# Q/K/V projections per quarter of the heads, and a prologue that runs under attention, in a fused attention and token-MLP kernel

## The chip, the cores and the metric

The kernel runs on one core of one Trainium2 chip. The metric is the device time of one execution in microseconds (us). All runs compared here are marked fast in the record, and each lists one core.

## The reference, cut to what matters

```python
xn = layernorm(x)                                    # x: [1, 2048, 512], bf16
# A: attention with 32 heads of width 16
q, k, v = split(xn @ wqkv)                           # wqkv: [512, 3*512]
o = softmax(q @ k.T * 16**-0.5) @ v                  # per head, 2048 x 2048 scores
a = o @ wo
# B: token MLP, along the 2048 tokens, with width F = 1376
h = layernorm(xn)
u = gelu(h.T @ w1 + b1)                              # tanh form
b = (u @ w2 + b2).T
out = x + a + b
```

The scores have 32 * 2048 * 2048 = 134 million elements, and each needs an exponential. That is the work which cannot be made smaller here.

## The kernel before

All engines get their instruction streams from one scheduling loop in Python. Scores are computed transposed (keys on partitions). One *period* of the loop is one key tile of 128 keys for 4 heads and 512 queries: four score matmuls that use 32 rows of TensorE each, two exponentials of 128x1024 on ScalarE, and four PV matmuls for the period two before. Sixteen periods make a *block* (4 heads, 512 queries), and there are 32 blocks. Scores go to three PSUM slots of two banks each, bank 6 takes PV, and bank 7 (`EX_BANK`) takes every other matmul: projections, MLP and output projection. Such extra work is queued, and each period takes up to `EXTRA_BUDGET` matmuls from the queue; a task that asks for more at once, as a Q projection with its 4, is taken whole when the period has taken nothing else yet.

```python
EXTRA_BUDGET = 3.0
...
for s_ in range(NT + 4):                 # prologue, 16 tiles of 128 tokens
    if s_ < NT:
        ln_stats(s_, 0)
        ...
    t = s_ - 1
    if 0 <= t < NT:
        ln_norm(t, 0); transpose_pe(t, t % 2)
    t = s_ - 2
    if 0 <= t < NT:
        transpose_copy(t, t % 2, "act")
        v_pe(t, 2 + (t % 2))             # V of all 32 heads
        if t % 4 == 3:
            kt_pe(0, t // 4, ...)        # K of head-quarter 0
    ...                                  # evacuations of stage s_ - 3
qt_block(0, EX_BANK, evac_eng="act")
...
def task_qt(b):                          # Q of one block: a burst of four matmuls
    yield 4.0                            # weights padded with zeros per head parity
    qt_block(b, EX_BANK)
...
while True:                              # one period
    score_group(period)                  # 4 matmuls into slots n % 3
    exp_pair(2 * period); exp_pair(2 * period + 1)
    pv_group(...)                        # of period - LAG
    ...                                  # extra work: at most EXTRA_BUDGET matmuls
```

After the last block, its head group is copied from PSUM, its denominators are broadcast and inverted in four pieces, and each piece is multiplied, projected, added and stored before the next is inverted.

The softmax here doesn't subtract the row's maximum and nothing guards it: scores larger than these inputs give would overflow.

Of the kernel before, what the change touches and what calls it, by code (L numbers as in the profile page):

```python
# [13 lines left out]
D = 512  # L14
# [18 lines left out]
EXTRA_BUDGET = 3.0  # L33
# [23 lines left out]
class Sched:  # L57
# [11 lines left out]
    def add(self, eng, fn, reads=(), writes=(), name="", dma=False, extra_deps=(), out_dma=False):  # L69
# [4 lines left out]
        for k in reads:  # L74
            w = self.last_writer.get(k)
            if w is not None:
                deps.add(w)
        for k in writes:
            w = self.last_writer.get(k)
            if w is not None:  # L80
                deps.add(w)
            for r in self.readers.get(k, ()):
                deps.add(r)
# [97 lines left out]
def bass_parallel_sum__softmax_full_mha__mixer_token_mlp__prompt_kernel(  # L181
# [18 lines left out]
    with ExitStack() as es:  # L200
# [18 lines left out]
        wq_pad = sb("wq_pad", [128, NCT, NG, 128], BF16)  # L219
# [54 lines left out]
        v17_main = V17[:, 0:NKT * H * 17].rearrange("p (n c) -> p n c", c=17)  # L274
        sc.add("dve", lambda e: e.memset(v17_main[:, :, 16:17], 1.0), writes=[("Vone",)])
        sc.add("dve", lambda e: e.memset(V17[:, NKT * H * 17:], 0.0), writes=[("Vpad",)])

        xsplits = [(0, 1), (1, 2), (2, 4), (4, 8), (8, 12), (12, 16)]
        for (a, b_) in xsplits:
            dma("sp", x_sb[:, a:b_, :],  # L280
                x2[128 * a:128 * b_, :].rearrange("(t p) d -> p t d", p=128),
                reads=[], writes=[("x", t) for t in range(a, b_)], name="ld_x")
            if a == 0:
                dma("sp", wqkv_sb[:], A_wqkv.rearrange("(ct p) n -> p ct n", p=128),
                    reads=[], writes=[("wqkv",)], name="ld_wqkv")
# [8 lines left out]

        def pool_wqpad_piece(i):
            if i < NCT:
                sc.add("pool", lambda e: e.memset(wq_pad[:, i, :, :], 0.0), writes=[("wq_pad_ct", i)])
            else:
                j = i - NCT
                e_, ct = divmod(j, NCT)  # L300
                src = wqkv_sb[:, ct, 0:D].rearrange("p (T r e d) -> p T r e d", T=4, r=4, e=2)[:, :, :, e_, :]
                dst = wq_pad[:, ct, :, :].rearrange("p (T e) (r f d) -> p T e r f d", e=2, r=4, f=2)[:, :, e_, :, e_, :]
                sc.add("pool", lambda e, dst=dst, src=src: e.tensor_copy(dst, src),
                       reads=[("wqkv",), ("wq_pad_ct", ct)], writes=[("wq_pad_ct", ct)] +
                       ([("wq_pad", g) for g in range(NG)] if j == 2 * NCT - 1 else []), name="wqpad")
# [58 lines left out]
        def kt_evac(T, c, bk, evac_eng):  # L364
            evac(evac_eng, KT[:, T, 512 * c:512 * (c + 1)], bank(bk), reads=[("bank", bk)], writes=[("KT", T, c)])

        def kt_pe(T, c, bk):
            for ct in range(NCT):
                sc.add("pe", lambda e, ct=ct: e.matmul(  # L369
                    bank(bk), lhsT=wqkv_sb[:, ct, D + 128 * T: D + 128 * T + 128],  # L370
                    rhs=xnT[:, ct, 512 * c:512 * (c + 1)], start=(ct == 0), stop=(ct == NCT - 1)),
                    reads=[("wqkv",)] + [("xnT", t) for t in range(4 * c, 4 * c + 4)], writes=[("bank", bk)])
# [6 lines left out]
        def qt_block(b, bk, evac_eng="dve"):  # L379
            qb, G = divmod(b, NG)  # L380
            slot = b % NQS
            for ct in range(NCT):
                sc.add("pe", lambda e, ct=ct: e.matmul(  # L383
                    bank(bk), lhsT=wq_pad[:, ct, G, :], rhs=xnT[:, ct, 512 * qb:512 * (qb + 1)],
                    start=(ct == 0), stop=(ct == NCT - 1)),
                    reads=[("wq_pad", G)] + [("xnT", t) for t in range(4 * qb, 4 * qb + 4)], writes=[("bank", bk)])
            evac(evac_eng, QT[:, slot, :], bank(bk), reads=[("bank", bk)], writes=[("QT", slot)])

        def v_tile(t, bk, evac_eng="dve"):
            v_pe(t, bk)  # L390
            v_evac(t, bk, evac_eng)

        def v_evac(t, bk, evac_eng):
            dst = V17[:, t * H * 17:(t + 1) * H * 17].rearrange("p (h c) -> p h c", c=17)[:, :, 0:16]
            src = bank(bk).rearrange("p (h d) -> p h d", d=16)
            evac(evac_eng, dst, src, reads=[("bank", bk)], writes=[("V", t)])

        def v_pe(t, bk):
            for ct in range(NCT):
                sc.add("pe", lambda e, ct=ct: e.matmul(  # L400
                    bank(bk), lhsT=xnT[:, ct, 128 * t:128 * (t + 1)], rhs=wqkv_sb[:, ct, 2 * D:3 * D],
                    start=(ct == 0), stop=(ct == NCT - 1)),
                    reads=[("wqkv",), ("xnT", t)], writes=[("bank", bk)])

        pool_piece = 0
        for s_ in range(NT + 4):
            if s_ < NT:
                ln_stats(s_, 0)
                if pool_piece < 3 * NCT:
                    pool_wqpad_piece(pool_piece)  # L410
                    pool_piece += 1
            t = s_ - 1
            if 0 <= t < NT:
                ln_norm(t, 0)
                transpose_pe(t, t % 2)
            t = s_ - 2
            if 0 <= t < NT:
                transpose_copy(t, t % 2, "act")
                v_pe(t, 2 + (t % 2))
                if t % 4 == 3:  # L420
                    kt_pe(0, t // 4, 4 + ((t // 4) % 2))
            t = s_ - 3
            if 0 <= t < NT:
                v_evac(t, 2 + (t % 2), "dve" if t % 2 == 1 else "act")
                if t % 4 == 3:
                    kt_evac(0, t // 4, 4 + ((t // 4) % 2), "act")
        while pool_piece < 3 * NCT:
            pool_wqpad_piece(pool_piece)
            pool_piece += 1
        qt_block(0, EX_BANK, evac_eng="act")  # L430
        late_consts()

        def task_ln2():
            for t in range(NT):
                yield 0.0
                ln_tile(t, 1)

        def task_qt(b):
            yield 4.0
            qt_block(b, EX_BANK)  # L440

        def task_kt(T):
            for c in range(4):
                yield 4.0
                kt_chunk(T, c, EX_BANK)
# [61 lines left out]
        def task_outproj(qb, sti):  # L507
# [3 lines left out]
            ng = NG - 1 if lastqb else NG  # L511
            for G in range(ng):
                yield 1.0
                sc.add("pe", lambda e, G=G: e.matmul(  # L514
# [17 lines left out]
        def final_tile(qb, sti):  # L532
            st = 4 * qb + sti
            par = qb % 2
            G = NG - 1
            bk = sti
            sc.add("pe", lambda e: e.matmul(
                bank(bk), lhsT=oT[:, par, G, 128 * sti:128 * (sti + 1)], rhs=wo_pad[:, G, :],
                start=True, stop=True),
                reads=[("oTc", par, G, sti), ("wo_pad", G)], writes=[("bank", bk)])  # L540
            final_store(st, bk)
            yield 0.0
# [6 lines left out]
        def task_epilogue_rest(b):  # L549
            qb, G = divmod(b, NG)  # L550
            eb = b % 2
            last = (b == NBLK - 1)
# [3 lines left out]
            for c in range(4):  # L556
# [4 lines left out]
                if last:  # L561
                    sc.add("dve", lambda e, cs=cs: e.tensor_tensor(oT[:, qb % 2, G, cs], OT32[:, eb, cs],
                                                                   denb[:, eb, cs], ALU.mult),
                           reads=[("OT32", eb), ("denb", eb, c)], writes=[("oTc", qb % 2, G, c)])
                    for _ in final_tile(qb, c):
                        pass
            if not last:
                yield 0.0
                sc.add("pool", lambda e: e.tensor_tensor(oT[:, qb % 2, G, :], OT32[:, eb, :], denb[:, eb, :], ALU.mult),  # L569
                       reads=[("OT32", eb)] + [("denb", eb, c) for c in range(4)],  # L570
                       writes=[("oTc", qb % 2, G, c) for c in range(4)])
# [9 lines left out]
        def score_group(g):  # L581
            b, kt, qb, G, T, e_ = blk_of(g)
            slot_q = b % NQS
            for r in range(4):
                n = 2 * g + r // 2
                s_ = n % 3
# [5 lines left out]
                    reads=[("KT", T, kt // 4), ("QT", slot_q)], writes=[("bank", bk)], name="sc")  # L592

        def exp_pair(n):
            s_ = n % 3
# [4 lines left out]
        def pv_group(g):  # L600
            b, kt, qb, G, T, e_ = blk_of(g)
            for r in range(4):
# [8 lines left out]
                    reads=[("V", kt), ("pT", buf), ("Vone",)] + ([("V", kt + 1)] if kt + 1 < NKT else [("Vpad",)]),  # L611
# [4 lines left out]

        sched_list = []
        for b in range(1, NBLK):
            sched_list.append((P(b - 1, 1), 0, "qt", b))
        for T in range(1, 4):  # L620
            sched_list.append((P(2 * T - 2, 2), 1, "kt", T))
        for ft in range(NFT):
            sched_list.append((P(1, 4) + 6 * ft, 2, "ut", ft))
        for st in range(NT):
            sched_list.append((P(1, 4) + 6 * NFT + 7 * st, 3, "yt", st))
        for qb in range(NQB):
            for sti in range(4):
                if qb < NQB - 1:
                    sched_list.append((P(8 * (qb + 1), 8) + 4 * sti, 4, "op", (qb, sti)))
                else:  # L630
                    sched_list.append((P(NBLK - 1, 8) + 2 * sti, 4, "op", (qb, sti)))
        sched_list.sort(key=lambda z: (z[0], z[1]))

        def start_task(kind, arg):
            if kind == "qt":
                return task_qt(arg)
            if kind == "kt":
                return task_kt(arg)
            if kind == "ut":
# [18 lines left out]
        free_tasks = [Task("ln2", None, task_ln2())]  # L658
# [5 lines left out]
        while True:  # L664
            if period == P(0, 8):
# [123 lines left out]
```

## Time and profile before

| what | before | where it is read |
|---|---|---|
| median time | 1042.1 us (4 runs), 1041.07 (13 runs) | timing runs |
| span of the profiled run | 1040.3 us | page |
| ScalarE busy | 967.0 us (93%) | page, part 1 |
| start of the first exponential | 44.43 us | ScalarE's timeline |
| ScalarE idle ahead of exponentials | 32.0 us | groups |
| end of the last exponential to the end | 15.1 us | ScalarE's timeline |

Lines of the page of the kernel before: busy time by engine, the clock row (the span in 40 slices, tenths of full clock), the chain of waits by engine and by line, and the group of the exponentials (busy us, mean ns of one | idle us ahead of them, and what ended it).

```profile
PE 893.7 (86%) x4833; PEld 211.2 (20%) x4896; DVE 294.9 (28%) x476; ACT 967.0 (93%) x1065; POOL 75.7 (7%) x116
PEclk9966888887899999965557755555555955555558
ACT 78%; PE 14%; DVE 4%; issue 1%; POOL 1%; DMA 1%; ACTq 0%; SPq 0%
L597 ACT ACTIVATE pT<-ps 128x1024 bf16<-128x1024 f32 x1024 | 946.4, 1255 | 32.0 <-PE ps L588 32.0
```

ScalarE is the limit (busy 967.0 of 1040.3 us). So the time is a sum along ScalarE: the start of the first exponential, the exponentials, the gaps between them, and what follows the last one. The mean of 1255 ns is the length of one record; records overlap, and back to back one starts every 0.92 us (32 take 29.44 us in the timeline below).

ScalarE's timeline of the kernel before shows the sum's terms (start us, duration us, group of adjacent instructions, and in brackets the idle time ahead and who ended it).

```profile
44.43 9.38 ACT L597 ACTIVATE pT<-ps 128x1024 bf16<-128x1024 f32 x10 [0.48 <-PE ps L588]
...
293.41 159.60 ACT L597 ACTIVATE pT<-ps 128x1024 bf16<-128x1024 f32 x174 [0.44 <-PE ps L588]
453.87 29.44 ACT L597 ACTIVATE pT<-ps 128x1024 bf16<-128x1024 f32 x32 [0.85 <-PE ps L588]
484.16 29.44 ACT L597 ACTIVATE pT<-ps 128x1024 bf16<-128x1024 f32 x32 [0.85 <-PE ps L588]
...
1014.09 11.11 ACT L597 ACTIVATE pT<-ps 128x1024 bf16<-128x1024 f32 x12 [0.55 <-PE ps L588]
```

From about 450 us on there is a gap of 0.85 us behind 16 of the 18 Q bursts, one burst per block of 32 exponentials, while in the 159.60 us before that there is none. The table of windows of the kernel before (window, its length; busy us and count of PE, PEld, DVE, ACT, POOL; then PEclk, DMA share, GB/s):

```profile
300.00:350.00 50.00, 46.28 (x293) 13.12 (x299) 17.74 (x28) 50.00 (x56) 2.54 (x2) 1.00 0.19 44
600.00:650.00 50.00, 45.12 (x216) 8.67 (x218) 10.83 (x16) 48.28 (x53) 2.53 (x2) 0.50 0.00 1
```

With MLP matmuls among the scores (300 to 350 us) the granted clock is 1.00, without them (600 to 650 us) 0.50. TensorE's timeline of the kernel before, around 451 us, shows what the Q burst does on the slow clock (0.50 from 450.8 to 453.3 us):

```profile
450.85 0.61 PE L607 MATMUL ps<-pT,V 128*32 128x512 bf16 x4
451.80 1.49 PE L383 MATMUL ps<-xnT,wq_pad 128*128 128x512 bf16 x3 [0.33 <-issue]
453.22 1.03 PE L588 MATMUL ps<-QT,KT 32*128 32x512 bf16 x6
```

L383 is the Q burst (one of its four records is missing). It stands between the PV matmuls and the next scores (L588), which start at 453.22; the next exponential could only start at 453.87, after its gap.

### The profile page before, as it was taken

To read this page: it belongs to the slowest core of one execution; us is meant where nothing else is said; L and a number is where in the kernel's file an instruction comes from. 1 tells how busy PE (TensorE), PEld (TensorE's weight loads), DVE (VectorE), ACT (ScalarE), POOL (GpSimd) and SP (SyncE) were. 2 spreads that over 40 slices of the span, in tenths; PEclk is the share of its full clock that TensorE was granted. 3 is DMA by queue.
4 is the path that set the end of the run, shared out by engine and by line. 5 is a ranking of instruction groups with operands and counts; after the bars stand their busy time and mean duration, and the time that the engine had idled before them with its cause. 6 is when DMAs were issued, how large, how long until landed. Compare 5 with 4: busy or idle time off the path is not lost.

```text
span 1040.3 us, 11570 instructions
## 1 busy us (share of the span) xinstructions
PE 893.7 (86%) x4833; PEld 211.2 (20%) x4896; DVE 294.9 (28%) x476; ACT 967.0 (93%) x1065; POOL 75.7 (7%) x116
## 2 busy tenths in 40 slices
PE   5777887888889999889988899888898899898895
PEld 2311221222222222211112211111111211111111
DVE  6654433343332223322201222221022222102214
ACT  3698999999999999999999999999999999999994
POOL 5431000000000000000000000000000000000000
PEclk9966888887899999965557755555555955555558
DMA  5020201011012111100000000000000000000000
GB/s 141 19 44 21 48 21 41 21 22 35 1 29 51 37 29 42 28 0 1 1 1 11 11 1 1 1 1 1 1 0 6 16 1 1 1 1 1 1 1 20
DMA packets 54372, 18.31 MB, mean 18 GB/s; under 512 B 49200, under 2 KB 53808, under 8 KB 54320
## 3 DMA queue, kind: packets, MB, share of 16 engines
q1 hardware_dynamic: 54320, 17.58, 7.1%
q8 instruction: 38, 0.62, 0.2%
q14 instruction: 14, 0.11, 0.0%
HBM read 15.47 MB, written 2.10 MB: 17 GB/s over the span
## 4 chain that ended last, share of the span: by engine, by line
ACT 78%; PE 14%; DVE 4%; issue 1%; POOL 1%; DMA 1%; ACTq 0%; SPq 0%
ACT pT L597 77%; PE ps L588 4%; PE ps L383 3%; PE ps L607 2%; PE ps L468 1%; DVE stats L323 1%; PE ps L400 1%; DVE big L338 1%; POOL mv L329 1%; PE ps L514 1%; DMA x_sb<-in_A_x_dram 1%; ACT ga_sb L483 1%; PE ps L369 1%; DVE mv L325 0%; PE ps L348 0%
## 5 line engine op out<-in xcount | busy, mean ns | idle before, releaser
L597 ACT ACTIVATE pT<-ps 128x1024 bf16<-128x1024 f32 x1024 | 946.4, 1255 | 32.0 <-PE ps L588 32.0
L588 PE MATMUL ps<-QT,KT 32*128 32x512 bf16 x2048 | 482.7, 511 | 99.7 <-ACT pT L597 65.4
L607 PE MATMUL ps<-pT,V 128*32 128x512 bf16 x2048 | 262.1, 514 | 2.2 <-DVE OT L546 1.9
L588 PEld LDWEIGHTS ps<-QT,KT 32*128 32x128 bf16 x2048 | 94.0, 96 | 510.7 <-ACT pT L597 461.4
L546 DVE COPY OT<-ps 128x512 f32<-128x512 f32 x32 | 22.1, 691 | 436.4 <-PE ps L607 436.3
L559 DVE RECIPROCAL denb<-denb 128x128 f32<-128x128 f32 x128 | 110.3, 915 | 0.9
L569 POOL TENSOR_TENSOR oT<-OT,denb 128x512 bf16<-128x512 f32 x31 | 39.3, 1267 | 880.9 <-DVE denb L559 880.9
L607 PEld LDWEIGHTS ps<-pT,V 128*32 128x32 bf16 x2048 | 53.0, 99 | 169.6 <-issue 166.4
L468 PE MATMUL ps<-big,w1blk 128*128 128x512 bf16 (+1 forms) x165 | 54.2, 434 | 2.5 <-issue 1.8
L383 PE MATMUL ps<-xnT,wq_pad 128*128 128x512 bf16 x101 | 43.2, 558 | 7.8 <-issue 7.8
L495 PE MATMUL ps<-gT,w2blk 128*128 128x512 bf16 (+1 forms) x165 | 47.1, 386 | 2.3 <-issue 1.9
L514 PE MATMUL ps<-wo_pad,oT 128*128 128x512 bf16 x115 | 36.0, 415 | 2.0 <-issue 1.8
L377 DVE CAST QT<-ps 128x512 bf16<-128x512 f32 x31 | 21.4, 691 | 35.9 <-PE ps L383 35.9
L500 DVE SCALAR_TENSOR_TENSOR big<-ps,x_sb 128x512 f32<-128x512 f32 x16 | 11.0, 690 | 66.9 <-PE ps L495 66.9
L473 DVE TENSOR_SCALAR u_sb<-ps,b1col 128x512 f32<-128x512 f32 (+1 forms) x11 | 8.2, 750 | 73.3 <-PE ps L468 73.3
L527 DVE TENSOR_TENSOR osb<-ps,big 128x512 bf16<-128x512 f32 x16 | 11.1, 691 | 57.7 <-PE ps L514 55.1
L376 ACT ACTIVATE xnT<-ps 128x512 bf16<-128x512 bf16 x16 | 9.5, 594 | 16.7 <-PE ps L348 16.7
L554 DVE STREAM_SHUFFLE denb<-OT 128x512 f32<-128x512 f32 x32 | 23.1, 721 | 0.0
L348 PE MATMUL ps<-ident,big 128*128 128x128 bf16 x64 | 7.4, 249 | 15.3 <-DVE big L338 15.2
L369 PE MATMUL ps<-xnT,wqkv_sb 128*128 128x512 bf16 x61 | 17.1, 397 | 3.9 <-DVE KT L377 3.2
L468 PEld LDWEIGHTS ps<-big,w1blk 128*128 128x128 bf16 (+1 forms) x176 | 14.0, 105 | 28.6 <-issue 20.5
L400 PE MATMUL ps<-wqkv_sb,xnT 128*128 128x512 bf16 x62 | 19.6, 450 | 0.1
(44 smaller groups left out, 205.1 us busy)
## 6 DMA issues: line engine op xcount, KB each, us to landing
w1blk<-in_B_w_dram SPq DMA_DIRECT2D x10, 512.0 KB, 4.1
w2blk<-in_B_w_dram SPq DMA_DIRECT2D x16, 320.0 KB, 3.3
out_dram<-osb SPq DMA_DIRECT2D x16, 128.0 KB, 1.7
wqkv_sb<-in_A_wqkv_dram SPq DMA_DIRECT2D x1, 1536.0 KB, 6.8
x_sb<-in_A_x_dram SPq DMA_DIRECT2D x3, 512.0 KB, 8.7
wo_pad<-in_A_wo_dram SPq DMA_DIRECT2D x8, 64.0 KB, 2.0
w2blk<-in_B_w_dram SPq DMA_DIRECT2D x16, 24.0 KB, 1.7
w1blk<-in_B_w_dram SPq DMA_DIRECT2D x1, 384.0 KB, 3.9
```

The lines of the kernel that those rows point to most:

```text
L369: sc.add("pe", lambda e, ct=ct: e.matmul(bank(bk), lhsT=wqkv_sb[:, ct, D + 128 * T: D + 128 * T + 128], rhs=xnT[:, ct, 512 * c:512 * (c + ...
L383: sc.add("pe", lambda e, ct=ct: e.matmul(bank(bk), lhsT=wq_pad[:, ct, G, :], rhs=xnT[:, ct, 512 * qb:512 * (qb + 1)], start=(ct == 0), sto ...
L400: sc.add("pe", lambda e, ct=ct: e.matmul(bank(bk), lhsT=xnT[:, ct, 128 * t:128 * (t + 1)], rhs=wqkv_sb[:, ct, 2 * D:3 * D], start=(ct == 0 ...
L468: sc.add("pe", lambda e, st=st: e.matmul(bank(EX_BANK)[0:m, :], lhsT=w1blk[:, slot, st, 0:m], rhs=h_sb[:, st, :], start=(st == 0), stop=(s ...
L495: sc.add("pe", lambda e, ft=ft, m=m: e.matmul(bank(EX_BANK), lhsT=w2blk[0:m, slot, ft, :], rhs=gT[0:m, ft, :], start=(ft == 0), stop=(ft = ...
L514: sc.add("pe", lambda e, G=G: e.matmul(bank(EX_BANK), lhsT=oT[:, par, G, 128 * sti:128 * (sti + 1)], rhs=wo_pad[:, G, :], start=(G == 0), ...
L554: sc.add("dve", lambda e: e.stream_shuffle(denb[:, eb, :], OT32[:, eb, :], [16] * 32), reads=[("OT32", eb)], writes=[("denb", eb, c) for c ...
L559: sc.add("dve", lambda e, cs=cs: e.reciprocal(denb[:, eb, cs], denb[:, eb, cs]), reads=[("denb", eb, c)], writes=[("denb", eb, c)])
L569: sc.add("pool", lambda e: e.tensor_tensor(oT[:, qb % 2, G, :], OT32[:, eb, :], denb[:, eb, :], ALU.mult), reads=[("OT32", eb)] + [("denb" ...
L588: sc.add("pe", lambda e, r=r, bk=bk: e.matmul(bank(bk), lhsT=KT[32 * r:32 * r + 32, T, 128 * kt:128 * (kt + 1)], rhs=QT[32 * r:32 * r + 32 ...
L597: sc.add("act", lambda e: e.activation(pT[:, buf, :], ps[:, s_ * 1024:(s_ + 1) * 1024], ACTF.Exp, scale=0.25), reads=[("bank", 2 * s_), (" ...
L607: sc.add("pe", lambda e, r=r, buf=buf, off=off: e.matmul(bank(PV_BANK)[32 * r:32 * r + 32, :], lhsT=V17[:, off:off + 32], rhs=pT[:, buf, 5 ...
```

## The change

The intent is to start attention early and to keep its feed even. Only head-quarter 0 of Q, K and V is projected before attention, for the first 4 token tiles; the other 12 tiles run inside block 0. The other quarters are queued as extra work. One Q projection serves two blocks, split by two masks instead of zero-padded weights, and is queued as two halves of two matmuls. The cap on extra work falls from 3 to 2 matmuls per period. The weights load in six pieces on a second queue. The tail is shortened. The K projections of later quarters are halved in the same way, the MLP starts about three blocks later, and the output projections move in the queue. The core of the diff:

```diff
-EXTRA_BUDGET = 3.0
+EXTRA_BUDGET = 2.0
 ...
+        ld_w(2, 0, 1)          # V, K, Q of quarter 0 first, on ScalarE's queue
+        ld_w(1, 0, 1)
+        ld_w(0, 0, 1)
+        ld_w(1, 1, 4)
+        ld_w(2, 1, 4)
+        ld_w(0, 1, 4)
 ...
+        def qt_proj_gen(qb, T, bk, act_first=False):
+            for ct in range(NCT):
+                if ct % 2 == 0:
+                    yield 2.0
+                sc.add("pe", ... lhsT=wqkv_sb[:, ct, 128 * T:128 * (T + 1)] ...)
+            yield 0.0
+            for e_ in range(2):                      # two blocks from one projection
+                ... e.tensor_scalar(QT[:, slot, :], bank(bk), qmask[:, e_:e_ + 1], None, ALU.mult)
 ...
+        NPRE = 4
+        def tb(t):
+            return t % 2 if t < NPRE else 4          # transposes inside block 0: one bank
+        def vb(t):
+            return 2 + (t % 2) if t < NPRE else 5    # V: one bank
+        def pro_stage(s_, pre):
+            ev = "act" if pre else "dve"             # inside block 0 VectorE empties all
+            ...  # t = s_-5: V and K out of PSUM; s_-4: K, Q, V matmuls; s_-3: transpose copy
+            ...  # s_-2: transposes; s_: statistics; s_-1: normalise
 ...
+        def pslot(n):
+            return n % 2 if n < 2 * NKT else n % 3   # two score slots in block 0
 ...
+            if period < NKT:
+                block0_work(period)
 ...
+        def tail_epilogue(b):
+            for sti in range(4):
+                final_pre(qb, sti)                   # last but one head group, ahead of time
+            ... stream_shuffle(denb[:, eb, :], bank(PV_BANK), ...)   # no copy of PSUM
+            recip_mult(0)
+            for c in range(1, 4):
+                recip_mult(c)
+                final_store(4 * qb + c - 1, c - 1)   # stores between the reciprocals
+            final_store(4 * qb + 3, 3)
```

## The prediction

> **What bounds the kernel now.** ScalarE. The page's groups show 1024 exponentials of 128x1024, 946.4 us busy, 0.924 us each back to back; ScalarE is busy 967 of 1040.3 us, and that line is 77% of the chain of waits. In ScalarE's timeline the rest is (1) a prologue: the first exponential starts at 44.43 us, after 16 tiles of LayerNorm, transposes, V and K; (2) 11 tanh between exponentials, about 0.52 us each, 6 us; (3) 32.0 us in 47 gaps, put down to score matmuls; (4) a tail from the last exponential's end at 1025.2 to 1040.3, 15 us.
>
> About 30 of the gaps are 0.85 us, one per block, where four Q-projection matmuls go in one burst. In the table of windows the granted clock is 0.50 to 0.53 where TensorE runs only scores and PV, 1.00 where it also has MLP matmuls. The burst starts on the slow clock and takes about 1.7 us, more than the score buffers' lead. [...]
>
> **What the change does.**
> - Attention starts once 4 of 16 tiles are projected, for head-quarter 0 alone. The gate is x tiles 4 to 7, whose statistics stand ahead of tile 3's normalisation on VectorE, at about 10 us. From there to the scores: 5 to 6 us by durations of this trace. First exponential at 16.5 us (14 to 20): minus 28 us.
> - The rest of the prologue moves into block 0. VectorE per tile: three evacuations and a LayerNorm, about 2.3 us, against 1.85 us for two exponentials, with only two score buffers instead of three. I expect 2.3 to 2.6 us for about 12 periods: plus 8 us of gaps (5 to 15).
> - One Q projection serves two blocks by masks (15 instead of 31), in halves of two matmuls; extras are capped at 2 per period instead of 3. A half (0.86 us on the slow clock) should fit the lead. MLP work queues up, so the clock stays up. Gaps after block 0: 4 us (1 to 9) instead of about 30.
> - The exponentials and tanh stay: 952 us.
> - Tail: one copy (0.74 us) gone, the last-but-one head group pre-accumulated, stores interleaved with reciprocals. VectorE's chain is about 9.8 us and the last store 2.4: 12.3 instead of 15.
>
> **Sum.** 16.5 + 952.4 + 8 + 4 + 12.3 = 993 us of span, plus 1.8 that the measured time has over the span: 995 us. Range 984 to 1010. Faster by over 2%: 0.95; within 2%: 0.045; slower by over 2%: 0.005.
>
> **What would show each step.** ScalarE's timeline: first exponential at 14 to 20 us; block 0 (32 exponentials) in 35 to 44 us instead of 29.6, with gaps put down to score matmuls and behind them VectorE copies; the 0.85 us gap per block gone; total idle of the exponential line after its start near 12 us instead of 32; last exponential to end near 12 us; VectorE nearly full in block 0. The exponential's busy time must stay at 946 us.
>
> **What would make it wrong.** Block 0 slower than thought: single transpose and V banks tie TensorE to VectorE within a period, and on the half clock a period may take 3 us (plus 8 us). [...] V projections or Q evacuations behind reciprocals stalling blocks 1 to 5. The two-matmul halves still costing some 0.3 us each on the half clock.

Two passages of the recorded prediction are cut where marked. Its 2.3 us of VectorE per tile and its 3 us per period on the half clock are estimates of mine; the text does not say from which durations.

## The result, and the profile after

The changed kernel takes 983.41 us in the median (8 runs, 980.70 to 985.68); the kernel before took 1041.07 us (13 runs, 1039.92 to 1043.50). The ratio is 0.944, with a 95% interval of 0.9427 to 0.9452. A ratio here is the mean time of one kernel's fast runs over that of the other's fast runs of the same rounds, so it is not quite the ratio of the medians. The prediction of 995 us had the direction, and 984 us as its lower end; the measured time is just outside.

The same lines of the page, of the changed kernel:

```profile
PE 825.8 (84%) x5019; PEld 209.0 (21%) x5084; DVE 306.3 (31%) x522; ACT 954.1 (97%) x1045; POOL 70.2 (7%) x110
PEclk8999869888887888889999999555965555555797
ACT 86%; PE 10%; DVE 2%; issue 1%; DMA 1%; ACTq 0%; SPq 0%; DVEq 0%
L757 ACT ACTIVATE pT<-ps 128x1024 bf16<-128x1024 f32 x1024 | 946.6, 1349 | 6.3 <-PE ps L748 4.4
```

The exponentials' own busy time is the same, and the idle time ahead of them fell from 32.0 to 6.3 us. ScalarE's timeline of the changed kernel:

```profile
16.05 5.80 ACT L757 ACTIVATE pT<-ps 128x1024 bf16<-128x1024 f32 x6 [0.32 <-PE ps L748]
23.14 1.94 ACT L757 ACTIVATE pT<-ps 128x1024 bf16<-128x1024 f32 x2 [1.29 <-PE ps L748]
25.40 157.01 ACT L757 ACTIVATE pT<-ps 128x1024 bf16<-128x1024 f32 x170 [0.33 <-PE ps L748]
...
420.49 262.92 ACT L757 ACTIVATE pT<-ps 128x1024 bf16<-128x1024 f32 x286 [0.60 <-PE ps L748]
683.84 235.10 ACT L757 ACTIVATE pT<-ps 128x1024 bf16<-128x1024 f32 x256 [0.43 <-PE ps L748]
919.37 51.44 ACT L757 ACTIVATE pT<-ps 128x1024 bf16<-128x1024 f32 x56 [0.43 <-PE ps L748]
```

The first exponential starts at 16.05 us; block 0 has gaps of 1.29 and 0.33 us; whole stretches of 256 and 286 exponentials run without a listed gap. Windows of the changed kernel:

```profile
500.00:550.00 50.00, 41.49 (x264) 10.80 (x269) 15.82 (x24) 50.00 (x56) 2.54 (x2) 1.00 0.13 29
800.00:850.00 50.00, 46.43 (x225) 8.67 (x222) 7.22 (x11) 49.99 (x56) 2.53 (x2) 0.50 0.00 1
```

The clock is still 0.50 where there are only scores and PV, but ScalarE is now busy 49.99 of 50 us there, against 48.28 before.

The sum along ScalarE, before and after, and as predicted. "Exponentials and tanh" is the time from the first exponential's start to the last one's end, less the gaps between them:

| term | before | after | change | predicted after |
|---|---|---|---|---|
| start of the first exponential | 44.4 | 16.05 | -28.4 | 16.5 |
| exponentials and tanh | 949.2 | 948.8 | -0.4 | 952.4 |
| gaps after the first exponential | 31.5 | 6.0 | -25.5 | 12 (8 in block 0, 4 later) |
| last exponential's end to the end | 15.1 | 11.4 | -3.7 | 12.3 |
| span | 1040.3 | 982.2 | -58.1 | 993.2 |

So two terms make up nearly all of the 11 us by which the prediction was too high: 3.6 us in the exponentials and tanh, and 6.0 us in the gaps.

### The profile page after: what moved, and what is told of

Same layout as the page of the kernel before. It is cut to its first block, busy times and chain, and to the rows that moved or that the text cites. A ratio compares the mean times of both kernels' runs of the same rounds, so it can differ in the third digit from the quotient of the medians.

```text
span 982.2 us, 11965 instructions
## 1 busy us (share of the span) xinstructions
PE 825.8 (84%) x5019; PEld 209.0 (21%) x5084; DVE 306.3 (31%) x522; ACT 954.1 (97%) x1045; POOL 70.2 (7%) x110
## 4 chain that ended last, share of the span: by engine, by line
ACT 86%; PE 10%; DVE 2%; issue 1%; DMA 1%; ACTq 0%; SPq 0%; DVEq 0%
ACT pT L757 86%; PE ps L748 4%; PE ps L767 2%; PE ps L425 1%; PE ps L605 1%; PE ps L632 1%; ACT ga_sb L620 1%; DMA x_sb<-in_A_x_dram 1%; PE ps L389 0%; DVE QT L438 0%; DVE denb L717 0%; PE ps L652 0%; PE ps L445 0%; PE ps L366 0%; DVE osb L665 0%
## 5 line engine op out<-in xcount | busy, mean ns | idle before, releaser
L757 ACT ACTIVATE pT<-ps 128x1024 bf16<-128x1024 f32 x1024 | 946.6, 1349 | 6.3 <-PE ps L748 4.4
L748 PE MATMUL ps<-QT,KT 32*128 32x512 bf16 x2048 | 447.7, 465 | 123.2 <-ACT pT L757 102.1
L767 PE MATMUL ps<-pT,V 128*32 128x512 bf16 x2048 | 241.3, 472 | 1.0 <-ACT pT L757 1.0
L632 PE MATMUL ps<-gT,w2blk 128*128 128x512 bf16 (+1 forms) x160 | 54.4, 407 | 3.4 <-issue 1.8
L438 DVE TENSOR_SCALAR QT<-ps,qmask 128x512 bf16<-128x512 f32 x30 | 21.2, 747 | 34.5 <-PE ps L425 34.5
L425 PE MATMUL ps<-xnT,wqkv_sb 128*128 128x512 bf16 x49 | 22.6, 535 | 2.8 <-issue 2.8
L415 DVE CAST V<-ps 128x128 bf16<-128x128 f32 (+1 forms) x26 | 12.4, 476 | 22.9 <-PE ps L569 22.2
L347 POOL TENSOR_TENSOR mv<-mv,mhalf 128x1 f32<-128x1 f32 x32 | 18.1, 567 | 2.7
L605 PEld LDWEIGHTS ps<-big,w1blk 128*128 128x128 bf16 (+1 forms) x176 | 10.7, 102 | 27.5 <-issue 23.9
L415 DVE CAST KT<-ps 128x128 bf16<-128x128 f32 (+1 forms) x26 | 12.2, 469 | 13.9 <-PE ps L407 8.5
L407 PE MATMUL ps<-xnT,wqkv_sb 128*128 128x512 bf16 x42 | 14.1, 409 | 2.7 <-DVE KT L415 1.6
```

Source lines behind the costliest of these rows:

```text
L415: return sc.add("dve", lambda e: e.tensor_copy(dst, src), reads=reads, writes=writes)
L425: sc.add("pe", lambda e, ct=ct: e.matmul(bank(bk), lhsT=wqkv_sb[:, ct, 128 * T:128 * (T + 1)], rhs=xnT[:, ct, 512 * qb:512 * (qb + 1)], st ...
L605: sc.add("pe", lambda e, st=st: e.matmul(bank(EX_BANK)[0:m, :], lhsT=w1blk[:, slot, st, 0:m], rhs=h_sb[:, st, :], start=(st == 0), stop=(s ...
L632: sc.add("pe", lambda e, ft=ft, m=m: e.matmul(bank(EX_BANK), lhsT=w2blk[0:m, slot, ft, :], rhs=gT[0:m, ft, :], start=(ft == 0), stop=(ft = ...
L748: sc.add("pe", lambda e, r=r, bk=bk: e.matmul(bank(bk), lhsT=KT[32 * r:32 * r + 32, T, 128 * kt:128 * (kt + 1)], rhs=QT[32 * r:32 * r + 32 ...
L757: sc.add("act", lambda e: e.activation(pT[:, buf, :], ps[:, s_ * 1024:(s_ + 1) * 1024], ACTF.Exp, scale=0.25), reads=[("bank", 2 * s_), (" ...
```

## The experiments

Names that begin with b_ are edits of the kernel before, those with a_ of the changed kernel. Each was correct unless said otherwise, and timed in rounds with the kernel before on the same chip; all ratios are against that kernel. The ratios of b_halves, b_warm2 and b_newtail lie within 2% of 1, but their intervals leave 1 out, so these small differences are real. Two theories about the gaps are at stake. One: a burst of extra matmuls on the slow clock lasts longer than the score buffers' lead, that is, than the scores already in PSUM keep ScalarE supplied. Its rivals: fewer projections (masks) are what counts, or a burst costs its gap on any clock.

### b_halves: the Q burst split, nothing else

```diff
-            yield 4.0
-            qt_block(b, EX_BANK)
+            for ct in range(NCT):
+                if ct % 2 == 0:
+                    yield 2.0
+                sc.add("pe", ...)        # the same matmuls, two per period
+            evac("dve", QT[:, slot, :], bank(EX_BANK), ...)
```

> The kernel before, with only its Q projections (still 31) split into two halves of two matmuls in two periods. Theory (the burst of four on the slow clock outlasts the score buffers' lead): the 0.85 us gap per block goes, ScalarE's gaps fall from 32 us to about 8 to 12, time 1017 to 1023. Rival (the number of projections, halved by the masks, is what counts, not the burst): gaps stay within 3 us of 32, time 1038 to 1042.

Measured: 1033.4 us, ratio 0.9907 (0.9886 to 0.9927), gaps 20.5 us. That is neither number. ScalarE's timeline of this run says why:

```profile
282.28 11.11 ACT L606 ACTIVATE pT<-ps 128x1024 bf16<-128x1024 f32 x12 [0.60 <-PE ps L597]
...
400.68 156.47 ACT L606 ACTIVATE pT<-ps 128x1024 bf16<-128x1024 f32 x170 [0.32 <-PE ps L597]
560.05 233.89 ACT L606 ACTIVATE pT<-ps 128x1024 bf16<-128x1024 f32 x254 [0.53 <-PE ps L597]
```

The gap of 0.85 us per block is gone where it came from Q alone, after 450 us, with all 31 projections still there. So the burst, not the number of projections, made those gaps. But about 16 us of gaps before 300 us remained, no less than before. Part of them are new. In three places, ahead of the gaps of 1.82, 0.97 and 1.83 us at 150.18, 211.50 and 247.09 us, an MLP matmul (L477) stands behind Q's second half in the same period and waits for VectorE to empty the one bank. TensorE's timeline at the first:

```profile
147.17 1.03 PE L444 MATMUL ps<-xnT,wq_pad 128*128 128x512 bf16 x2
149.00 0.61 PE L477 MATMUL ps<-big,w1blk 128*128 128x512 bf16 x1 [0.79 <-DVE QT L377]
```

Of the rest, about 5 us stand behind MLP matmuls on the half clock (as in the kernel before the gap of 0.43 us at 103.87 us, at a clock of 0.50), and 2.4 us behind K's bursts (0.89 us twice at clock 1.00, where TensorE had waited 1.13 and 1.36 us for VectorE to empty the bank).

### b_halves_cap2: the cap as well

```diff
-EXTRA_BUDGET = 3.0
+EXTRA_BUDGET = 2.0
```

> As b_halves, and the cap on extra matmuls per period is 2 instead of 3, everything else as before. Theory: the remaining gaps are the MLP's bursts of three on the slow clock, so they go too: gaps 2 to 6 us, time 1010 to 1016, first exponential still at 44.4. Rival (gaps of blocks 1 to 9 come from other waits, VectorE evacuations for one): gaps stay at 8 to 12 and the time equals b_halves.

Measured: 1020.09 us, ratio 0.9787 (0.9766 to 0.9809), gaps 8.2 us, first exponential at 43.73 us. The cap took another 12 us of gaps, so the rival as it was put (time as in b_halves) falls; the theory's own numbers were a little too good. But it had a grain of truth, for the cap did two things: it made the MLP's bursts smaller, and as Q's half now fills a period's budget, no matmul follows it to wait for the bank (11 such waits of about 0.79 us in b_halves, none here). How much each is worth was not told apart. The cap also has a price: the tail takes 17.3 us in this run, from the last exponential's end at 1000.48 us to the span of 1017.8, as output projections are left over for it. Two small settings of the queue, without any change of prologue, masks or tail, give 22 of the 58 us.

### b_warm and b_warm2: the bursts stay, the clock is kept up by useless work

```diff
+            idle_for = 0 if bank_q else idle_for + 1
+            if idle_for >= 3 and period < NGRP:
+                for _ in range(2):       # useless, overwritten later
+                    sc.add("pe", lambda e: e.matmul(bank(EX_BANK), lhsT=ident[:], rhs=xnT[:, 0, 0:512], ...))
```

> The kernel before, its bursts of four untouched, with two useless matmuls per period wherever no other extra work has been queued for three periods, so that TensorE does more work but its clock may stay up. Theory (the slow clock is what makes the burst too long): granted clock near 0.95 after 300 us and the 0.85 us gaps go in that stretch (20 of them, 17 us), time 1020 to 1027 although TensorE has more to do. Rival (a burst of four always costs 0.85 us): the gaps stay and time is 1040 or more.

Measured: 1041.39 us, ratio 0.9982 (0.9961 to 1.0004): same. The clock rose to 0.97 to 1.00 after 400 us (windows of 100 us) and a gap of 0.75 us behind most Q bursts stayed, as the rival had it. TensorE's timeline shows a fault of the edit:

```profile
486.56 1.04 PE L383 MATMUL ps<-xnT,wq_pad 128*128 128x512 bf16 x4
...
488.38 0.60 PE L727 MATMUL ps<-xnT,ident 128*128 128x512 bf16 x2 [0.79 <-DVE QT L377]
488.92 0.40 PE L588 MATMUL ps<-QT,KT 32*128 32x512 bf16 x4
```

The burst takes 1.04 us on the fast clock, but two useless matmuls (L727) stood right behind it in the same period and waited 0.79 us for VectorE to empty the bank. The mended version puts none within three periods of other extra work:

```diff
-            idle_for = 0 if bank_q else idle_for + 1
+            idle_for = 0 if bank_q or len(sc.streams["pe"]) > n_pe else idle_for + 1
```

> b_warm mended: there the two useless matmuls also stood right behind each Q burst and waited 0.79 us for VectorE to empty its bank. Now none stands within three periods of other extra work; the bursts of four stay. Theory (slow clock makes the burst too long): granted clock near 0.95 after 300 us, the gap per block after 300 us falls from 0.85 to 0 to 0.2 us, time 1024 to 1030. Rival (a burst of four costs its 0.75 to 0.85 us on any clock): the gaps stay, time 1040 or more.

Measured: 1025.44 us, ratio 0.9834 (0.9807 to 0.9861). The window and the gaps of this run:

```profile
700.00:800.00 100.00, 84.30 (x528) 21.50 (x536) 17.05 (x26) 99.62 (x110) 3.79 (x3) 0.93 0.01 2
L597 ACT ACTIVATE pT<-ps 128x1024 bf16<-128x1024 f32 x1024 | 945.5, 1308 | 16.5 <-PE ps L588 15.7
```

The kernel got 17.8 us faster by doing more work on TensorE: the 0.85 us gaps after 450 us are gone with the bursts of four intact. Two listed gaps, of 0.23 and 0.25 us, remain there; the 15 us of gaps before 300 us stayed. The slow clock is a necessary part of the cause of the gaps after 450 us, as the burst's size is (b_halves). How long the clock took to come up can be read in this trace: the first useless matmuls of a block stand at 486.19 us, and four score matmuls take 0.61 us (those that end at 489.83) and later 0.40 us (those that start at 491.28), so the clock came up 3.6 to 5.1 us after the first useless matmul.

### a_burst4: the changed kernel with bursts of four again

```diff
-                if ct % 2 == 0:
-                    yield 2.0
+                if ct == 0:
+                    yield 4.0
```

> The changed kernel with its 15 later Q projections as bursts of four again. Theory: bursts that fall on the slow clock cost about 0.85 us each, those on the fast clock nothing: gaps rise from 6.3 to 10 to 18 us, the additional ones mainly after 600 us; time 986 to 996. Rival (masks alone removed the gaps): time within 2 us of 983.

Measured: 992.06 us, ratio 0.9507 (0.9485 to 0.9529), gaps 15.5 us: 9 us more gaps for 15 bursts. The masks alone did not remove them. About half of the additional gaps lie between 180 and 380 us, not mainly after 600 as I had expected. TensorE's timeline has bursts on both clocks (the second with one record missing):

```profile
487.03 1.04 PE L425 MATMUL ps<-xnT,wqkv_sb 128*128 128x512 bf16 x4
892.07 1.49 PE L425 MATMUL ps<-xnT,wqkv_sb 128*128 128x512 bf16 x3 [0.33 <-issue]
```

Taken burst by burst, with the clock granted during each, this trace settles the cause of the Q gaps: 8 of the 15 bursts stand at 0.50, and each is followed by a gap of 0.86 us; 7 stand at 1.00, and no gap follows. The kernel before tells the same: of its 31 later bursts 23 stand at 0.50, and 22 of them are followed by a gap of 0.84 to 0.86 us (the other by 0.29); behind the 8 at 1.00 there is none.

### a_stats2: more VectorE work in block 0

```diff
                 ln_stats(t, 0)
+                if not pre:
+                    sc.add("dve", lambda e, t=t: e.bn_stats(stats2[:], x_sb[:, t, :]), ...)
```

> The changed kernel with the statistics instruction of the ten tiles normalised in block 0 issued twice (0.69 us more of VectorE per tile). The prediction's mechanism (VectorE's work per tile against the 1.84 us of two exponentials sets the period of block 0; only its size was overstated at 2.3 us where the trace shows about 1.9): period of about 2.5 us for ten tiles, 5 to 7 us more gaps, time 988 to 991. Rival (TensorE on the slow clock makes the gaps of block 0, VectorE has slack): time within 2 us of 983.

Measured: 985.43 us, ratio 0.9468 (0.9452 to 0.9484), whose interval touches that of the changed kernel; gaps 7.8 us. That is between the theory's numbers and the rival's. The traces decide. VectorE's timeline of the changed kernel for one tile in block 0, and then of this run:

```profile
28.93 0.42 DVE L415 COPY xnT<-ps 128x512 bf16<-128x512 bf16 x1
29.27 0.69 DVE L341 BATCH_NORM_STATS2 stats<-x_sb 128x6 f32<-128x512 bf16 x1
29.99 0.18 DVE L343 BATCH_NORM_AGGREGATE mv<-stats 128x2 f32<-128x6 f32 x1
30.09 0.38 DVE L356 TENSOR_SCALAR big<-x_sb,mv 128x512 bf16<-128x512 bf16 x1
30.39 0.28 DVE L415 CAST KT<-ps 128x128 bf16<-128x128 f32 x1
30.59 0.28 DVE L415 CAST V<-ps 128x128 bf16<-128x128 f32 x1
30.78 0.41 DVE L415 COPY xnT<-ps 128x512 bf16<-128x512 bf16 x1
```

```profile
28.38 0.41 DVE L416 COPY xnT<-ps 128x512 bf16<-128x512 bf16 x1
...
30.82 0.41 DVE L416 COPY xnT<-ps 128x512 bf16<-128x512 bf16 x1
```

In the changed kernel a tile takes 1.85 us here (28.93 to 30.78; 1.93 on average from 28.93 to 36.63), about the time of two exponentials (1.84 us). With the statistics doubled it takes 2.44 us, and four gaps of about 0.50 us appear, 2.43 us apart, while the clock is 1.00 (windows from 28 to 40 us). ScalarE's timeline of this run:

```profile
32.05 1.94 ACT L761 ACTIVATE pT<-ps 128x1024 bf16<-128x1024 f32 x2 [0.50 <-PE ps L752]
34.48 1.94 ACT L761 ACTIVATE pT<-ps 128x1024 bf16<-128x1024 f32 x2 [0.50 <-PE ps L752]
```

So the prediction's mechanism is there: work of VectorE above ScalarE's pace turns into gaps. But from the first exponential to the 33rd (start times in the trace) this run takes 33.3 us against 32.0, not 5 to 7 us more: it pays in four periods, not in ten. Why it does not pay in all ten was not shown.

### a_pre16: no overlap with attention

```diff
-        NPRE = 4
+        NPRE = 16
 ...
-                if t < NPRE:
+                if t < 4:
                     qt0_tile_pe(t)
```

> The changed kernel with all 16 tiles done ahead of the first exponential (no overlap with attention), still only head-quarter 0. Theory (the gain at the start is mostly the overlap): the first exponential moves from 16.05 to 31 to 36 us and the gaps of block 0 (about 2 us) vanish, time 996 to 1002. Rival (the gain comes from projecting a quarter instead of all of V, and from the split loads): first exponential at 20 to 25 us, time 986 to 991.

Measured: 996.97 us, ratio 0.9579 (0.9564 to 0.9594). ScalarE's timeline of this run:

```profile
30.20 126.03 ACT L757 ACTIVATE pT<-ps 128x1024 bf16<-128x1024 f32 x136 [0.27 <-PE ps L748]
```

The first exponential starts at 30.20 us, a little earlier than the theory's range and far from the rival's. Half of the gain at the start comes from the overlap (30.20 to 16.05) and half from the rest of the prologue's change (44.43 to 30.20): a quarter of V instead of all of it, and the loads in pieces; these two were not told apart. Block 0 takes 29.8 us here from the first exponential to the 33rd, against 32.0 with the overlap (31.4 in a_again, the same kernel once more), so the overlap costs 1.6 to 2.2 us in block 0 and saves 14.15 us ahead of it. This run too has only two score buffers in block 0, so these alone cost nothing: from 32 to 48 us ScalarE is busy 4.00 of every 4 us.

### a_notanh: what the tanh cost (a wrong result)

```diff
-            sc.add("act", lambda e: e.activation(ga_sb[...], ga_sb[...], ACTF.Tanh, scale=GELU_C), ...)
-            yield 0.0
```

> The changed kernel without its 11 tanh (a wrong result on purpose). The prediction added 6 us for tanh to the exponentials' busy time. If that busy time already spans the tanh, as overlapping records suggest, the exponentials' busy time falls from 946.6 to about 940 and the time by 5 to 6.5 us, to 977 to 978.5. Rival (the tanh hide in the exponentials' pipeline and cost about 2 us, as the sum of ScalarE's busy time says): time falls by 1 to 3 us and the busy time of the exponentials stays at 946.

Measured: 976.62 us, ratio 0.9384 (0.9363 to 0.9406). The group of the exponentials:

```profile
L754 ACT ACTIVATE pT<-ps 128x1024 bf16<-128x1024 f32 x1024 | 943.0, 1386 | 8.0 <-PE ps L745 6.0
```

The exponentials alone take 943.0 us here (first start to last end, less gaps) against 948.8 with tanh. (The record lists this run as correct all the same: its check did not notice the missing tanh.) So the 11 tanh do cost 5.8 us, 0.52 each, but 3.6 us of it is already in the exponentials' busy time of 946.6, because records overlap. The busy time fell by less than I wrote (to 943.0, not 940).

### b_newtail: the tail alone

```diff
-            ng = NG - 1 if lastqb else NG
+            ng = NG - 2 if lastqb else NG
 ...
+                        tail_epilogue(b)     # as in the changed kernel
```

> The kernel before with only the new tail (last head group read straight from PSUM, last but one added ahead, stores between the reciprocals). Theory: the time from the last exponential's end to the end falls from 15.1 to about 11.4 us as in the changed kernel, time 1036.5 to 1039.5. Rival (the shorter tail is a by-product of the other parts): 1040 or more.

Measured: 1039.51 us, ratio 0.9966 (0.9941 to 0.9991); the last exponential ends at 1024.49 us and the span is 1035.7 us, so the tail is 11.2 us instead of 15.1. The kernel before took 1043.23 us in the same rounds. The tail's gain is its own; its three parts were not told apart.

### a_warm0, a_warm1, a_warm2 and a_again: TensorE's clock at the start

In block 0 the changed kernel's listed gaps stand where the clock is low: 0.50 between 20 and 24 us. With the clock as one theory and VectorE and the loads as the other, these runs put useless 128-column matmuls into the prologue.

```diff
+        warm(40)                             # all three
         for s_ in range(NSTG_PRE):
             pro_stage(s_, True)
+            if s_ == 2: warm(20)             # all three
+            elif s_ > 2: warm(12)            # a_warm1; in a_warm2 only for 2 < s_ < 7
 ...
+            if period < 2: warm(8)           # a_warm1 and a_warm2, in block 0
```

> The changed kernel with 60 useless 128-column matmuls in the first 8 us, while TensorE waits for data. Theory (from 8.3 us to the first exponential, and in the first 9 us of block 0, TensorE on the slow clock is the limit): first exponential at 13.5 to 15 instead of 16.05, the gaps of block 0 at 20 to 25 us go, time 979 to 981. Rival (VectorE and the loads set the start): first exponential within 0.5 us of 16.05, time within 1.5 us of 983.

> The changed kernel with more useless matmuls ahead of attention than a_warm0 (there the clock fell back to half between 16 and 22 us): 12 after each later stage, 8 in each of the first two periods of block 0. Theory (the gap of 1.3 us near 22 us comes from the slow clock): clock 1.0 from 6 us on, no gap over 0.4 us in block 0, first exponential at 14.3 to 15.3, time 979 to 981. Rival (it comes from the wait for the statistics and copies of VectorE): the gap stays though the clock is up.

> As a_warm1 but without the 24 useless matmuls right ahead of the first scores, which there held the first exponential up by 1.03 us. If the slow clock is all that the start of the changed kernel still loses besides VectorE's work: first exponential at 14.2 to 15.0 us, 32 exponentials in 29.3 us as in a_warm1 (32.0 in the changed kernel), time 3 to 4 us below a_again. Rival (VectorE and the loads hold the start, block 0 slows again once the fillers ahead of it are gone): 32 exponentials in 30.5 us or more, time within 2 us of a_again.

> The changed kernel itself, unchanged, on the same chip and in the same rounds as a_warm2, as its control: 982 to 985 us.

| run | time | ratio, 95% | first exponential | first to 33rd |
|---|---|---|---|---|
| a_warm0 | 981.13 | 0.943 (0.941 to 0.945) | 15.23 | 31.8 |
| a_warm1 | 982.26 | 0.9417 (0.9395 to 0.944) | 15.68 | 30.2 |
| a_warm2 | 983.25 | 0.9424 (0.9406 to 0.9442) | 16.04 | 30.5 |
| a_again | 983.70 | 0.9437 (0.9424 to 0.945) | 16.20 | 31.4 |

Windows of the changed kernel and of a_warm1 between 20 and 24 us:

```profile
20.00:24.00 4.00, 3.99 (x31) 2.05 (x32) 2.83 (x9) 2.71 (x3) 0.93 (x3) 0.50 1.26 227
```

```profile
20.00:24.00 4.00, 3.78 (x44) 1.93 (x40) 3.75 (x13) 3.92 (x5) 1.71 (x4) 1.00 1.11 208
```

With the clock up, ScalarE is busy 3.92 of 4 us there instead of 2.71, and block 0 takes 0.9 to 1.8 us less (the 29.3 us that the text of a_warm2 gives for a_warm1 is 30.2 by start times). So the slow clock, not VectorE, made the large gaps of block 0. In a_warm0 the clock fell back to half as block 0 began (0.50 between 16 and 20 us), and a gap of 1.35 us stayed. In a_warm1_pool below, with the fillers of a_warm1, the clock still fell to 0.59 between 20 and 24 us, and a gap of 1.07 us came back at 23.10 us. But the first exponential did not come earlier. It lay between 15.11 and 16.20 us in five runs whose prologue was the same (the changed kernel, a_again, a_burst4, a_notanh, a_stats2), and the statistics of the third tile, which wait for the load, started between 5.74 and 7.70 us in them. In a_warm2 they started at 7.07 us, and the first exponential at 16.04. In the end none of the three versions beats a_again outside the intervals, so none is offered as an improvement.

### a_warm1_pool: one reciprocal of the tail on GpSimd

```diff
-                sc.add("dve", ... e.reciprocal(denb[:, eb, cs], ...))       # for c = 3
+            sc.add("pool", ... e.tensor_tensor(denb[:, eb, 384:512], denb[:, eb, 384:512], neg1[:], ALU.pow))
```

> As a_warm1, and the last of the four reciprocals of the tail goes to GpSimd beside VectorE's first three. If GpSimd does it in under 4 us, VectorE's chain in the tail is 0.9 us shorter: tail 10.3 to 10.7 instead of 11.4, time 978 to 980.5. If GpSimd takes longer, the tail gets longer by the excess.

Measured: 996.83 us, ratio 0.956 (0.9537 to 0.9583), 15 us slower than a_warm1. GpSimd's timeline of this run:

```profile
969.99 20.79 POOL L739 TENSOR_TENSOR denb<-denb,neg 128x128 f32<-128x128 f32 x1 [20.18 <-DVE denb L726]
```

GpSimd needs 20.79 us for 128x128 fp32 where VectorE's reciprocal needs 0.94, and 0.29 for the multiplication of the same shape behind it. This fails, and clearly. GpSimd's power of 128x1 fp32 with an exponent of -0.5, in the LayerNorm of the changed kernel, takes 0.57 us.

## Why the prediction was right or wrong

- **The bound and the start** were right. The first exponential was predicted at 16.5 us and came at 16.05. The named gate (the load of tiles 4 to 7) was not shown: the third tile's statistics waited for their load in all of the runs looked at, those of the fifth (the first of tiles 4 to 7) only in some. So the number says little for the gate.
- **Gaps after block 0** were right in size: 4 us predicted. The trace of the changed kernel has 4.05 us: of the 6.3 us, 0.32 stand ahead of the first exponential and 1.96 in the rest of block 0 (1.62 in listed gaps, the rest in smaller ones). The cause was right too for the Q gaps: bursts on the slow clock. b_halves and b_warm2 each removed them after 450 us by another means. What was wrong was to give nearly all of the 32 us to Q: 22 gaps of about 0.85 us, 19 us in all, follow Q bursts, not 30. Of the gap reduction that b_halves_cap2 shows, 11.5 us came from Q's halves and 12.3 us from the cap, which the prediction named without a share of its own. That the total came out right is therefore partly luck.
- **"Plus 8 us of gaps (5 to 15)" in block 0 is the step that failed most.** The gaps there are 1.96 us, and block 0 lost 1.6 to 2.2 us against a_pre16: about 6 us less than predicted. Two sizes in it were wrong. First, VectorE's 2.3 us per tile: it was 1.85 to 2.00, 1.93 on average, with all three evacuations in 0.73 to 0.79 us (start to start) where I had put about 1.1, an estimate (the prediction does not itemise this). For the copy of the 16-bit transposes I had in mind ScalarE's 0.60 us, and VectorE took 0.42. A copy of 128x512 from PSUM takes VectorE 0.42 us in the changed kernel where the data are bf16, and 0.69 where they are fp32; the kernel before has only fp32 ones on VectorE, so its trace could not show the first. Second, I charged the excess to about 12 periods; a_stats2 shows that even at 2.44 us per tile only four gaps of 0.50 us follow. The mechanism was off as well: at 1.93 us VectorE nearly keeps pace with two exponentials, and what loss there is in block 0 is mainly the slow clock at its start (0.4 us of gaps are left with the clock up, in a_warm1), which the prediction had named only as a risk.
- **"The exponentials and tanh stay: 952 us" was the second step that failed.** They did stay, but at 948.8 us. I added the tanh's 6 us to a busy time that held 3.6 us of it already (a_notanh).
- **The tail** was predicted at 12.3 us and measured 11.4. b_newtail (11.2) shows that the new tail does it, not which of its parts.

Together, 6.0 + 3.6 + 0.9 + 0.45 = 11 us of span, and the range of 984 to 1010 us missed 983.41 by 0.6 us. These four errors had the same sign, which a range built around their sum did not allow for.

Left open: how much of the start's 14.2 us without overlap is the quarter of V and how much the loads; and what would bring the first exponential below 15 us.

## What to carry to other kernels

When one engine is the limit, write the time as a sum along that engine (start, work, gaps, tail) from its timeline, and check that the terms add up to the span before changing any; busy times of groups whose records overlap must not be added. In this kernel the gaps of the saturated engine depended less on the amount of side work than on how it was grouped: two matmuls per period instead of bursts of three or four, with no other change, gave 22 us, and useless work that kept TensorE's clock up gave nearly 18. Overload of a helper engine need not cost its full excess: here 0.6 us too much of VectorE in each of ten periods cost four gaps of 0.50 us. A high busy share of TensorE did not by itself go with a high clock: with scores and PV alone its records cover 46.43 of 50 us and the clock is 0.50 (changed kernel, 800 to 850 us); with two matmuls of 128x512 more per period, in b_warm2, they cover 84.30 of 100 us and it is 0.93 (700 to 800 us). The added matmuls are 128*128 on the page, the scores 32*128 and PV 128*32; which of these differences sets the clock, no run here shows.
